# Replacing two triangular inverses through DRAM by products of repeated squares on TensorE, at the start of a recurrent kernel

## Chip, cores, metric

One core of one Trainium2 chip. The metric is the device time of one execution in microseconds (us), median of several runs. Before the prediction the kernel took 842.51 us (three runs, 840.56 to 845.51).

## The reference, cut to what matters

```python
# r, k, v, w, a, b: (4 batches, 8 heads, 768 steps, 40)
for t in range(S):
    y[:, :, t] = np.einsum('bhd,bhde->bhe', rt, state)
    Sa = np.einsum('bhde,bhe->bhd', state, at)
    state_decay = state * wt[:, :, None, :] - np.einsum('bhd,bhe->bhde', Sa, bt)
    state = state_decay + np.einsum('bhd,bhe->bhde', vt, kt)
# y becomes x: (3072 tokens, 320)
h = x @ w_in                                        # 320 x 2048
g = 0.5 * h * (1.0 + erf(h * inv_sqrt2))
out = (g @ w_out).astype(np.float32)                # 2048 x 320
```

The kernel works through the 768 steps in 12 chunks of 64. In each chunk the recurrence becomes products of 64 by 64 matrices and one inverse: with a strictly triangular matrix N of each head and batch (32 of them), it needs T = 1 + N + N² + … + N⁶³. The dense part (x @ w_in, GELU, @ w_out) follows chunk by chunk. The weights arrive in 64 bits and are converted to float32 on the chip, piece by piece.

## The kernel before: the parts concerned

An inverse is made in 32 by 32 blocks. N is stored to DRAM and fetched back with one block a partition, and one engine (VectorE or GpSimd) solves column by column. The result goes through DRAM again, and a *corner* on TensorE joins the blocks.

```python
def start_inverse(c, eng, place=None):
    ...
    for par in range(2):
        nc.sync.dma_start(out=Nb[par * n:(par + 1) * n], in_=blk)
    ...
    def columns():
        for j in range(BL - 1):                      # 31 columns, two instructions each
            ...
            eng.tensor_tensor(t, W[...], Nb[...], ALU.mult)
            eng.tensor_tensor(W[:, :rows, j + 1:], W[:, :rows, j + 1:], t, ALU.add)
            yield
```

Each group of head products is 32 matmuls of 64 by 64 or less, one for each head and batch. They use 64 by 64 corners of the array. On all four corners a group takes 1.1 us at full clock here. So up to four matmuls run side by side. Each float32 matmul leaves two records in the trace, so a group shows as x64:

```python
def mm(o, lhsT, rhs, first=True):
    nc.tensor.matmul(o, lhsT, rhs, start=first, stop=True, skip_group_check=True)
```

The order of each engine is the order of the program. QY is the pair of groups that gives a chunk's outputs and its new state. A *piece* is one of the parts in which the weights are converted: ten of w_in (5 blocks in 2 column halves) and 16 of w_out, the "second weights". The start reads (cut):

```python
make_N(0)
inverse = start_inverse(0, nc.vector)
...
make_N(1)
inverse_1 = start_inverse(1, nc.gpsimd, ...)
...
corner(0); joined(0)
...
first_pieces((2, 3, 4), nc.vector)      # conversion of w_in
...
make_QY(0, 0); make_QY(0, 1); store_inverse(1); outputs(0)
pieces.append(mlp(0))                   # dense part of chunk 0, handed out by fill()
...
corner(1); turn_state(); joined(1)
...
make_N(2); run(start_inverse(2, nc.gpsimd))
```

## Time and profile before

| | before |
|---|---|
| median | 842.51 us |
| span of the profiled execution | 848.1 us |
| first dense product starts | 125.09 us |
| N product of chunk 3 (the *mark*) | 226.37 us |
| from the mark to the end | 621.7 us |

PE is TensorE, DVE VectorE, ACT ScalarE, POOL GpSimd, and SPq the queue that issues the transfers.

Before the first dense product TensorE has a single pause that nothing in the profile ends (start, duration, and in brackets the pause):

```profile
82.90 2.86 PE L96 MATMUL QY<-VR,ks 64*64 64x104 f32 x58 [2.48 <-issue]
```

### The profile page before, as it was taken

Reading aid. Unit: us, or ns where it says so; the run is one execution under the profiler, and the core shown is the slowest. Engines: PE = TensorE matmul, PEld = TensorE weight load, DVE = VectorE, ACT = ScalarE, POOL = GpSimd, SP = SyncE. Lnnn points to the kernel's source line nnn. Section 1 sums busy time; section 2 is a strip of 40 time slices with the busy share of each in tenths; the row PEclk is TensorE's granted clock in tenths of the full one; section 3 lists DMA queues with packets and bytes.
Section 4 is the critical chain, followed back from the end, with each engine's and each line's share of the span. In section 5 each row is a group of like instructions: output and inputs, shape, how many; then the busy total and the mean of one; then the engine's idle time right before and its main releaser. Section 6 shows DMA issues by size and latency. Waiting matters only on the chain.

```text
span 848.1 us, 29196 instructions
## 1 busy us (share of the span) xinstructions
PE 734.3 (87%) x13256; PEld 600.9 (71%) x13256; DVE 295.1 (35%) x459; ACT 222.8 (26%) x257; POOL 311.7 (37%) x778
## 2 busy tenths in 40 slices
PE   4445379685799999999999999998999999989997
PEld 3334368463787887887787877877877877868785
DVE  2765453956223323232232333233233133211100
ACT  2321145222223232223223232331332322202010
POOL 4138000751057075182281281380570750820000
PEclk9975659876899999999899999998999999999999
DMA  7956583382272262532722622722722622020000
GB/s 127 116 104 138 83 125 100 96 143 66 38 121 40 57 100 52 86 65 45 112 38 46 103 55 46 114 39 45 126 46 48 110 52 47 4 53 11 22 12 15
DMA packets 250252, 60.36 MB, mean 71 GB/s; under 512 B 236240, under 2 KB 245968, under 8 KB 250128
## 3 DMA queue, kind: packets, MB, share of 16 engines
q1 hardware_dynamic: 249800, 58.17, 39.5%
q8 instruction: 104, 1.70, 0.9%
q10 hardware_dynamic: 328, 0.33, 0.2%
q14 instruction: 20, 0.16, 0.1%
HBM read 44.30 MB, written 10.22 MB: 64 GB/s over the span
## 4 chain that ended last, share of the span: by engine, by line
PE 65%; DMA 10%; DVE 8%; POOL 6%; SPq 5%; issue 4%; ACT 2%; ACTq 0%; DVEq 0%; POOLq 0%
PE ph L641 22%; PE po L649 17%; PE QY L96 4%; POOL W L461 3%; POOL tmp L459 3%; PE J L96 2%; DMA inv<-W 2%; SPq L608 2%; PE vT_ps L331 2%; PE kT_ps L331 1%; PE saT_ps L96 1%; PE M_ps L96 1%; DMA Nb<-N 1%; PE tn_ps L331 1%; PE RV_ps L96 1%
## 5 line engine op out<-in xcount | busy, mean ns | idle before, releaser
L649 PE MATMUL po<-w_out_sb,gt 128*128 128x320 f32 x768 | 223.8, 445 | 16.3 <-DVE w_out_sb L243 15.2
L641 PE MATMUL ph<-xt,w_in_sb 64*128 64x256 f32 x1920 | 228.4, 390 | 2.0 <-issue 1.8
L459 POOL TENSOR_TENSOR tmp<-W,Nb 128x126 f32<-128x126 f32 (+22 forms) x310 | 114.0, 368 | 281.6 <-DMA Nb<-N 258.1
L641 PEld LDWEIGHTS ph<-xt,w_in_sb 64*128 64x128 f32 x1920 | 188.2, 192 | 27.3 <-issue 4.1
L649 PEld LDWEIGHTS po<-w_out_sb,gt 128*128 128x128 f32 x768 | 144.9, 194 | 80.5 <-DVE w_out_sb L243 21.8
L461 POOL TENSOR_TENSOR W<-W,tmp 128x126 f32<-128x126 f32 (+22 forms) x310 | 123.6, 399 | 24.3
L643 ACT ACTIVATE gt<-ph 128x1024 f32<-128x1024 f32 x48 | 49.1, 1023 | 177.6 <-PE ph L641 177.5
L653 DVE COPY os<-po 128x320 f32<-128x320 f32 x24 | 11.8, 491 | 131.2 <-PE po L649 123.6
L351 POOL TENSOR_TENSOR ks<-k_raw,part 128x640 f32<-128x640 f32 x12 | 22.5, 1875 | 66.0 <-ACT part L323 44.8
L598 DVE TENSOR_TENSOR y<-QY,y 128x512 f32<-128x512 f32 x22 | 15.1, 685 | 74.4 <-PE QY L96 74.4
L96 PE MATMUL J<-L,N 32*32 32x32 f32 x768 | 10.3, 208 | 31.8 <-DVE L L498 31.8
L383 DVE TENSOR_TENSOR VR<-RV_ps,upper 128x1024 f32<-128x1024 f32 x12 | 14.7, 1223 | 58.6 <-PE RV_ps L96 58.6
L96 PEld LDWEIGHTS J<-L,N 32*32 32x32 f32 x768 | 9.1, 120 | 36.5 <-issue 36.4
L383 DVE TENSOR_TENSOR SM<-M_ps,upper 128x1024 f32<-128x1024 f32 x12 | 14.7, 1224 | 56.4 <-PE M_ps L96 56.4
L383 DVE TENSOR_TENSOR A<-A_ps,upper 128x1024 f32<-128x1024 f32 x12 | 14.7, 1223 | 54.9 <-PE A_ps L96 54.9
L96 PE MATMUL cum<-w_raw,cum_m 128*128 128x320 f32 x48 | 19.6, 538 | 15.7 <-ACT w_raw L313 15.7
L236 ACT ACTIVATE power<-power,rebias 128x320 uint32<-128x320 uint32 (+1 forms) x26 | 15.8, 622 | 52.7 <-DVE power L235 42.3
L643 ACT ACT_TABLE_LOAD x11 | 14.1, 1283 | 57.6 <-PE ph L641 57.6
L433 ACT COPY avs<-av 128x640 f32<-128x640 f32 x12 | 8.3, 692 | 73.5 <-PE av L96 73.5
L331 PE MATMUL vT_ps<-ident,v_pad 128*128 128x128 f32 x96 | 16.0, 323 | 12.3 <-DMA v_pad<-in_v_dram 12.3
L362 DVE TENSOR_TENSOR aT<-aT_ps,wpT 128x1024 f32<-128x1024 f32 x12 | 14.7, 1224 | 27.6 <-ACT wpT L360 21.3
L377 DVE COPY vT<-vT_ps 128x1024 f32<-128x1024 f32 x10 | 12.2, 1224 | 34.2 <-PE vT_ps L331 34.2
(123 smaller groups left out, 959.3 us busy)
## 6 DMA issues: line engine op xcount, KB each, us to landing
Nb<-N SPq DMA_DIRECT2D x22, 256.0 KB
w_raw<-in_w_dram SPq DMA_DIRECT2D x24, 160.0 KB
b_raw<-in_b_dram SPq DMA_DIRECT2D x24, 160.0 KB
k_raw<-in_k_dram SPq DMA_DIRECT2D x24, 160.0 KB
a_pad<-in_a_dram SPq DMA_DIRECT2D x24, 160.0 KB
v_pad<-in_v_dram SPq DMA_DIRECT2D x48, 80.0 KB
r_pad<-in_r_dram SPq DMA_DIRECT2D x48, 80.0 KB
out_dram<-os SPq DMA_DIRECT2D x48, 80.0 KB
```

The costliest lines, as they stand in the source:

```text
L96: nc.tensor.matmul(o, lhsT, rhs, start=first, stop=True, skip_group_check=True)
L236: nc.scalar.activation(power, power, ACT.Relu, bias=rebias, scale=8.0)
L331: nc.tensor.transpose(pt[:, g, n], src(g, n), ident)
L351: nc.gpsimd.tensor_tensor(ks[:, :, :, :D], raws.pop((c, "k")), rwv, ALU.mult)
L383: nc.vector.tensor_tensor(to, pt, upper.unsqueeze(1).to_broadcast([P, 2 * G * NP, C]), ALU.mult)
L459: eng.tensor_tensor(t, W[:, :rows, j:j + 1].to_broadcast([P, rows, rest]), Nb[:, j:j + 1, j + 1:].to_broadcast([P, rows, rest]), ALU.mult)
L461: eng.tensor_tensor(W[:, :rows, j + 1:], W[:, :rows, j + 1:], t, ALU.add)
L598: nc.vector.tensor_tensor(y2, Y, y2, ALU.add)
L608: eng.dma_start(out=xt[own + n * i:own + n * (i + 1), NP], in_=xt[other + REST:other + D, i])
L641: nc.tensor.matmul(ph[:, x, s], w_in_sb[half(x), kt, p * P:(p + 1) * P], xt[half(x), kt], start=kt == 0, stop=kt == NK - 1)
L643: nc.scalar.activation(gt[:, 4 * q:4 * q + 4].rearrange("p (s x) t -> p x s t", x=2), ph, ACT.Gelu)
L649: nc.tensor.matmul(po[:, g], gt[:, f, g * P:(g + 1) * P], w_out_sb[:, f], start=f == 0, stop=f == NF - 1)
```

## The change

The intent: the inverses of chunks 0 and 1 stand in front of everything else. Write the same sum as a product, T = (1 + N)(1 + N²)(1 + N⁴)…(1 + N³²), and do it on TensorE, which is half idle there, with no trip through DRAM. The inputs of chunk 1 come at once, and the first weights are loaded and converted by column halves, so that the first dense product needs only the first halves.

```diff
+    def crossed(name, *pairs):
+        o = duo(name).rearrange("p h (n t) -> p h n t", n=NB)
+        for l, r_ in pairs:
+            for n in range(NB):                     # 8
+                for h in range(2):
+                    for s in range(2):
+                        m = s * NB + n
+                        mm(o[half(s), h, n], ident[half(h), half(h)] if l is None else l[half(h), m], r_[half(h), m],
+                           n == 0 and l is pairs[0][0])
+    def straight(name, l, r_, col): ...             # the same on two of the four corners, columns from col on
+    def doubled(c):
+        nc.scalar.copy(UA, crossed("U2", (L1, U1)))
+        nc.vector.tensor_copy(LA, crossed("L2", (U1, L1)))
+        yield
+        nc.vector.tensor_tensor(X, crossed("T1", (None, U1)), every(eye), ALU.add)
+        yield
+        ...                                         # U4 L4, T2, U8 L8, T4, L16, T8
+        nc.vector.tensor_tensor(T[:, :, 16:], straight("T16", LB, T, 16), T[:, :, 16:], ALU.add)
+        nc.scalar.copy(UB[:, :, 32:], straight("Y16", LB, T, 32))
+        nc.vector.tensor_tensor(T[:, :, 32:], straight("T32", LB, UB, 32), T[:, :, 32:], ALU.add)
@@ the program's order, cut
-    make_N(0)
-    inverse = start_inverse(0, nc.vector)
+    make_N(0, False)
+    powers = doubled(0)
+    doubling(1)                                     # steps of it lie between the other groups
...
-    inverse_1 = start_inverse(1, nc.gpsimd, (...))
-    first_pieces((2, 3, 4), nc.vector)
+    first_pieces((0, 1, 2, 3, 4), 0, nc.gpsimd)     # first column halves
...
+    powers = doubled(1)
...
+    first_pieces((4, 0, 1, 2, 3), 1, nc.gpsimd)     # second column halves
...
+    make_saT(1)
     make_N(2)
     run(start_inverse(2, nc.gpsimd))
+    second_pieces(range(NF), nc.vector)
     seconds(1)                                      # the step that finishes the tenth piece of w_in
```

## The prediction

> **What bounds the kernel now.** I read the page's forty slices first, then the busy time in stretches, then each engine's instructions in order of time, with the chain that ended last beside them. A slice is 21.2 us.
>
> ```profile
> PE   4445379685799999999999999998999999989997
> POOL 4138000751057075182281281380570750820000
> ```
>
> From the twelfth slice on TensorE is nine tenths busy or more; before that it is not. The stretches give the size:
>
> ```profile
> 20.00:40.00 20.00, 8.11 (x28) 6.01 (x28) 15.44 (x39) 6.41 (x8) 3.12 (x6) 1.00 1.01 123
> 60.00:80.00 20.00, 9.07 (x322) 8.12 (x325) 10.24 (x15) 4.19 (x7) 17.10 (x38) 0.50 0.65 130
> 80.00:100.00 20.00, 6.09 (x144) 5.46 (x136) 13.22 (x23) 2.95 (x4) 4.31 (x10) 0.67 0.42 74
> 200.00:220.00 20.00, 12.08 (x114) 10.10 (x114) 6.57 (x13) 3.98 (x5) 0.77 (x3) 0.60 0.26 52
> 240.00:260.00 20.00, 20.00 (x485) 17.12 (x482) 5.22 (x7) 7.17 (x8) 16.20 (x42) 1.00 0.59 86
> ```
>
> The second figure is TensorE's busy time. Over the eleven stretches to 220 us it adds up to 132.8, so 87 us are idle; from 226 us on there is nearly nothing to win. I take the start of chunk 3's N product (226.37 us) as the mark: both kernels do the same from there on, some 616 us of the 842.5. So the question is how much earlier the changed kernel reaches this mark.
>
> TensorE's own order shows the waits on the way (start, duration, and in brackets the idle time with what ended it):
>
> ```profile
> 68.64 1.08 PE L96 MATMUL J<-L,N 32*32 32x32 f32 x64 [11.41 <-DVE L L498]
> 100.87 1.94 PE L331 MATMUL vT_ps<-ident,v_pad 128*128 128x128 f32 x8 [12.30 <-DMA v_pad<-in_v_dram]
> 125.09 7.28 PE L641 MATMUL ph<-xt,w_in_sb 64*128 64x256 f32 x40
> 142.75 4.59 PE L641 MATMUL ph<-xt,w_in_sb 64*128 64x256 f32 x40
> 164.84 1.43 PE L649 MATMUL po<-w_out_sb,gt 128*128 128x320 f32 x2 [4.91 <-DVE w_out_sb L243]
> 215.26 1.08 PE L96 MATMUL J<-L,N 32*32 32x32 f32 x64 [5.08 <-DVE L L498]
> 226.37 1.16 PE L96 MATMUL N_ps<-aT,nT 40*64 40x64 f32 x64
> ```
>
> First the inverse of chunk 0 (through DRAM and on VectorE) and chunk 1's late inputs hold it up, then the conversion of the second weights, then chunk 2's inverse coming back from DRAM. The dense block of chunk 0 starts at 125.1. GpSimd's order holds chunk 2's inverse:
>
> ```profile
> 151.38 0.24 POOL L459 TENSOR_TENSOR tmp<-W,Nb 128x31 f32<-128x31 f32 x1 [22.10 <-DMA Nb<-N]
> 181.39 0.36 POOL L461 TENSOR_TENSOR W<-W,tmp 128x16 f32<-128x16 f32 x1
> 299.65 0.24 POOL L459 TENSOR_TENSOR tmp<-W,Nb 128x31 f32<-128x31 f32 x1 [25.82 <-DMA Nb<-N]
> ```
>
> It takes 62 instructions and 30.4 us here, and 28.4 later (299.65 to 328.1). Between the mask of N (done at 143.1) and the first of them lie 8.3 us of store and fetch.
>
> **What the Trainium skill says.** "TensorE: Matmul & The Clock Gate", Part 1, has the array at half clock until about 3.4 us of sustained work, and back there after an idle window of that length. The trace agrees on the fall: after 4.91 us idle a pair of output matmuls takes 1.43 us, after 1.72 us idle 0.81. It agrees less on the rise: at 123 to 129 us some 6 us of unbroken work were needed. The same page, Part 3, says that matmuls on separate strips of the array run at once; 64 records of a 64 by 64 group take 1.1 us warm here and 1.95 cold, thus 17 ns a record. Its table at the top calls GpSimd's queue strictly first in, first out; in the trace nothing overtakes on that engine, and my main argument rests on it. "DMA: Bandwidth & Descriptors", Specifications, wants at least 512 bytes a descriptor for full rate; 236,240 of the 250,252 packets here are smaller, and the first four inputs (1.31 MB) landed by 12.2 us, some 2.3 us each.
>
> **The change, part by part.**
>
> *Removed:* for chunks 0 and 1 the two stores and fetches, 62 VectorE and 62 GpSimd instructions, and the corner products (some 2 us of TensorE each).
>
> *Added:* 18 groups of 32 small matmuls per chunk: 36 x 1.1 = 40 us warm, 70 cold, less 4 for the corners. Each step ends in a copy out of PSUM (1.02 us ScalarE, 1.22 VectorE), and handovers cost under 0.1 us (cum ends 8.82, its copy starts 8.86).
>
> *Chunk 0.* Inputs at 2.3 us each: w of both chunks by 7.8, b, a, k of chunk 0 by 14.7, chunk 1's by 21.6, v and r by 26.2, then 3.1 MB of first weights by about 48. Eight warming matmuls from 3.5 us, then sums and transposes without a gap: the array should be warm by 10. N and L products end near 17.6, their two masks at 19.3. Then the changed order of TensorE, group by group at 1.1 (transposes 0.9): U2, L2, chunk 1's three transposes, T1, U4, L4 end at 28; N, L of chunk 1 at 30; T2 32; k, v, r 35; U8, L8 37; RV, T4, A, L16, T8, av at 45.6. T16, Y16, T32 each wait for a copy, some 2.2 us apiece: sap ends near 54 (before: 74.5). VectorE's conversions between them are the likeliest delay.
>
> *Chunk 1.* From there to the first dense product TensorE has 38 us of groups, with ScalarE 32 us of copies, logs, table loads and conversions in strict order beside it. I allow 5 us for waits: first dense product at **97** (before: 125.1). So 28 us won.
>
> *And lost again.* The ten pieces of first weights now end in two GpSimd instructions each. The order of the changed GpSimd has nine pieces before chunk 2's inverse and the **tenth behind its 62 instructions**. The third dense product needs that piece. So: first dense product 4.5, two groups 2.2, mask 1.4: 105. Plus 8.3 for store and fetch, 28.4 for the inverse, some 2.7 for two instructions on 128 by 512 (from 1.57 for 128 by 640): **144**. Before, the third dense product started at 142.75. The whole lead is gone: TensorE idles some 32 us, from about 112 to 144, and VectorE's second conversion stands behind it too, as it needs the same piece's buffer.
>
> *After it.* Third product 5.5 (half cold) and two QY groups 3.4: chunk 1's QY ends at T = 153 (before 157.0). Then 13.5 of 16 second-weight pieces are still to convert, at 0.32 + 0.32 + 0.48 + 0.48 + 0.49 = 2.1 us: 28.4; state and outputs 5.4, two masks 2.4, a copy 0.8: 37. Their raw data are issued behind the output copies (6.7 us of issue) and chunk 3's loads (7 us), so I add 5: the last piece at T + 42 (before T + 47.5, with 11 pieces left). From there: rest of the third output product, corners, four transposes (3.6), fourth output product (4.5), joining: 11 us, where before it took 22, as three cold transposes (5.5) came after it and the inverse was waited for (5.1). Now the inverse is back long before. Mark at T + 53 = **206**, that is 20 us earlier. 842.5 - 20 = **823 us**.
>
> **The rivals.**
>
> *No stall.* If the tenth piece were done in time, the third product would start near 113, the mark be near 175, and the time near 792. For it: the author meant to hand over a lead of 28 us. Against: program order on GpSimd, which no wait can change. I give it 5%.
>
> *The new matmuls become the bound.* If gaps between dependent steps keep the array cold, chunk 0 ends near 60 and the first dense product near 107; all later marks shift by 10: 833 us. For it: between 100 and 117 us before, cold groups with gaps of 0.7 to 1.4 us stayed cold. Against: the warming matmuls and the interleaved work of the other chunk. 25%.
>
> *Transfers bound the start.* All of chunk 1's inputs go ahead of the weights, and the last weights land near 48, the first of them at 32. Their conversion starts near 45 at the earliest, so this should be hidden; raw data of the second half have 15 us to spare. If not, 5 to 8 us: 830. 10%.
>
> *Faster tail of the prologue.* If the conversions run freely after QY, at VectorE's pace, 5 us less: 818.
>
> **Range and chances.** The limit for 2% is 825.7 us, close to my number. The stall ties the mark to the first dense product: each microsecond by which this comes earlier or later goes through in full. I am unsure of it by some 8 us, of the part after QY by 6. That gives 806 to 838 for 8 in 10. Faster by over 2%: 0.57; within 2%: 0.41; slower: 0.02, as the prologue would have to lose 17 us beyond what it wins.
>
> **What would show it.** The first dense product near 97 us with a gap of about 30 us before the third, ended by a GpSimd instruction that writes the first weights; chunk 2's inverse on GpSimd right before this, unbroken; chunk 0's groups at 1.1 us from 10 us on; sap of chunk 0 near 54; no wait for chunk 2's inverse before its corner; the mark near 206, and the same length after it. I am wrong if the third dense product follows the second by less than 10 us, if the groups of chunk 0 last 1.9 us, or if the conversions after QY take over 48 us, as then they and not the stall set the end of the prologue.

## More of the kernel before

The page's headline, instruction queue and chain of work that ended last.

"Issue" is time in which an engine waited for nothing that the profile shows; q8 is a queue of instructions.

```profile
span 848.1 us, 29196 instructions
...
q8 instruction: 104, 1.70, 0.9%
...
PE 65%; DMA 10%; DVE 8%; POOL 6%; SPq 5%; issue 4%; ACT 2%; ACTq 0%; DVEq 0%; POOLq 0%
```

The page counts 13,256 matmul records and as many weight loads for TensorE. These 26,512 instructions in blocks of 256 are 103.6 blocks, and q8 shows 104 packets of 16 KB (1.70 MB). So q8 carries TensorE's instructions, 256 in a packet, and 128 matmul records with their weight loads use one up.

## The result, and the profile after

| | before | after |
|---|---|---|
| median (same chip) | 843.5 us | 886.58 us |
| span of the profiled execution | 848.1 us | 885.5 us |
| first dense product | 125.09 us | 141.61 us |
| third dense product | 142.75 us | 154.90 us, then again from 188.09 |
| mark | 226.37 us | 268.44 us |
| mark to the end | 621.7 us | 617.1 us |

The ratio after to before is 1.0506, 95% interval 1.0458 to 1.0553: slower by 5%. Every ratio here is the mean time of one kernel's fast runs over that of the kernel before in the same rounds, so it is not quite the ratio of the medians. One of the four runs after was slow (900.84 us) and doesn't count; the profiled one was fast.

From the mark on nothing is lost, so the whole loss lies before it. The page after; the two rows of digits answer to those of the prediction:

```profile
span 885.5 us, 33267 instructions
...
PE   6678769055769999999899999999999998989997
...
POOL 4004213640102714807418247066083480630000
...
q8 instruction: 120, 1.97, 1.0%
...
PE 59%; issue 10%; POOL 9%; SPq 8%; DMA 7%; DVE 5%; ACT 1%; POOLq 0%; DVEq 0%; ACTq 0%
```

TensorE starts busier than before (667876 against 444537), then there is a 0: the eighth slice, where GpSimd shows a 6. And "issue" went from 4% to 10% of the chain. So three questions: what the zero is, what the issue time is, and what happens after the zero. The busy times in stretches (PE, weight loads, DVE, ACT, POOL; then clock, DMA share, GB/s):

```profile
20.00:40.00 20.00, 13.21 (x511) 12.57 (x511) 7.99 (x7) 4.06 (x4) 2.39 (x3) 0.84 0.71 149
60.00:80.00 20.00, 14.69 (x429) 13.87 (x425) 6.34 (x12) 5.66 (x9) 5.08 (x4) 0.67 0.33 60
80.00:100.00 20.00, 14.19 (x593) 13.56 (x590) 8.60 (x11) 7.68 (x12) 8.79 (x8) 0.76 0.46 109
160.00:180.00 20.00, 0.00 (x0) 0.00 (x0) 0.00 (x0) 0.00 (x0) 16.63 (x44) 0.50 0.00 0
```

Between 20 and 100 us TensorE is busy for some 70% of the time. There is work, but no engine in the table is full and neither is the DMA. Some of TensorE's instructions, in order of time, show why (start, duration, and in brackets the idle time and what ended it):

```profile
18.56 0.89 PE L97 MATMUL U<-N,gt 64*64 64x64 f32 x38 [1.55 <-DVE gt L408]
20.93 1.01 PE L97 MATMUL U<-N,gt 64*64 64x64 f32 x26 [1.48 <-issue]
42.07 1.76 PE L97 MATMUL T<-T,ident 64*64 64x64 f32 x51 [5.43 <-issue]
66.50 3.32 PE L97 MATMUL T<-Tt,gt 64*64 64x48 f32 x64 [0.25 <-ACT Tt L519]
79.70 1.95 PE L97 MATMUL sap<-avs,Tt 64*64 64x40 f32 x64 [0.79 <-DVE Tt L525]
116.23 0.85 PE L97 MATMUL A_ps<-aT,kT 40*64 40x64 f32 x42 [1.91 <-issue]
120.66 0.85 PE L97 MATMUL T<-T,LA 64*64 64x64 f32 x41 [2.34 <-issue]
141.61 4.59 PE L731 MATMUL ph<-xt,w_in_sb 64*128 64x256 f32 x40
188.09 5.81 PE L731 MATMUL ph<-xt,w_in_sb 64*128 64x256 f32 x28 [31.62 <-POOL w_in_sb L259]
250.33 1.94 PE L353 MATMUL nT_ps<-ident,nb 128*128 128x128 f32 x8 [7.61 <-DVE nb L372]
```

Three things are to be seen.

First, TensorE pauses *in the middle of a group*: the group U is cut into 38 and 26 records by 1.48 us with nothing to wait for. Before its first dense product it has 16 such pauses, 27.2 us in sum; the kernel before had one of 2.48 us in that part. I counted the records up to each: 220, 475, 603, 731, 985, 1113, 1241, 1368, 1751, 2007, and so on. They lie 128 records apart, or a multiple of it, give or take one that the trace misses: 256 instructions, one packet of q8. (After: 15,326 records with their loads are 119.7 blocks, and q8 has 120.) Where two pauses lie one block apart, the groups behind them start 3.4 to 4.8 us after each other, and once 7.6. The profile has no name for the wait, but its spacing is that of the blocks in which instructions arrive.

Second, the predicted stall: 31.62 us before the third dense product, ended by GpSimd. GpSimd's order at its end:

```profile
158.46 0.24 POOL L550 TENSOR_TENSOR tmp<-W,Nb 128x31 f32<-128x31 f32 x1 [10.50 <-DMA Nb<-N]
...
185.24 0.23 POOL L552 TENSOR_TENSOR W<-W,tmp 128x16 f32<-128x16 f32 x1
185.42 1.27 POOL L258 TENSOR_TENSOR mant<-mant,w_out_sb 128x512 f32<-128x512 f32 x1
186.77 1.26 POOL L259 TENSOR_TENSOR w_in_sb<-mant,power 128x512 f32<-128x512 f32 x1
```

Chunk 2's inverse runs from 158.46 to 185.47, and the tenth piece of w_in stands behind it.

Third, from the end of chunk 1's QY (196.9) to the mark (268.4) pass 71.5 us. The chain of work that ended last shows what holds this stretch (start, duration, what):

```profile
203.57 0.81 SPq L696
...
217.73 0.67 SPq L133
218.45 4.03 DMA spare_raw<-in_moe_w_out_dram
223.97 0.50 DVE w_out_sb L254
```

The issuing queue works from 203.57 to 218.45 on the output copies and chunk 3's inputs. Only then comes the load of the next second weights, and 4.03 us more pass until they land.

### The profile page after: what moved, and what is told of

Its sections match the earlier page's. It is cut to its first block, busy times and chain, and to the rows that moved or that the text cites. A ratio compares the mean times of both kernels' runs of the same rounds, so it can differ in the third digit from the quotient of the medians.

```text
span 885.5 us, 33267 instructions
## 1 busy us (share of the span) xinstructions
PE 768.0 (87%) x15326; PEld 638.4 (72%) x15326; DVE 271.0 (31%) x384; ACT 241.4 (27%) x285; POOL 306.0 (35%) x737
## 4 chain that ended last, share of the span: by engine, by line
PE 59%; issue 10%; POOL 9%; SPq 8%; DMA 7%; DVE 5%; ACT 1%; POOLq 0%; DVEq 0%; ACTq 0%
PE ph L731 20%; PE po L739 16%; POOL W L552 4%; POOL tmp L550 4%; PE QY L97 4%; SPq L133 2%; SPq L699 2%; DMA inv<-W 2%; PE J L97 2%; DMA Nb<-N 2%; PE kT_ps L353 1%; PE T L97 1%; PE tn_ps L353 1%; PE A_ps L97 1%; PE M_ps L97 1%
## 5 line engine op out<-in xcount | busy, mean ns | idle before, releaser
L731 PE MATMUL ph<-xt,w_in_sb 64*128 64x256 f32 x1920 | 225.4, 388 | 32.3 <-POOL w_in_sb L259 31.6
L731 PEld LDWEIGHTS ph<-xt,w_in_sb 64*128 64x128 f32 x1920 | 185.6, 191 | 57.2 <-POOL w_in_sb L259 32.0
L552 POOL TENSOR_TENSOR W<-W,tmp 128x126 f32<-128x126 f32 (+22 forms) x310 | 119.3, 385 | 24.3
L373 POOL TENSOR_TENSOR ks<-k_raw,part 128x640 f32<-128x640 f32 x11 | 19.2, 1744 | 71.0 <-ACT part L345 65.9
L258 POOL TENSOR_TENSOR mant<-mant,w_out_sb 128x512 f32<-128x512 f32 x9 | 11.6, 1284 | 84.1 <-ACT mant L257 84.1
L97 PE MATMUL RV_ps<-rT,vT 40*64 40x64 f32 x768 | 15.0, 229 | 7.6 <-ACT rT L401 5.8
L97 PEld LDWEIGHTS J<-L,N 32*32 32x32 f32 x640 | 6.7, 105 | 20.3 <-issue 20.3
L97 PEld LDWEIGHTS RV_ps<-rT,vT 40*64 40x64 f32 x768 | 13.3, 142 | 11.0 <-ACT rT L401 6.0
L97 PE MATMUL J<-L,N 32*32 32x32 f32 x640 | 7.6, 193 | 15.5 <-DVE L L589 15.5
L97 PEld LDWEIGHTS QY<-VR,ks 64*64 64x64 f32 x768 | 18.3, 137 | 3.6 <-issue 3.6
```

The source lines that it names most:

```text
L373: nc.gpsimd.tensor_tensor(ks[:, :, :, :D], raws.pop((c, "k")), rwv, ALU.mult)
L731: nc.tensor.matmul(ph[:, x, s], w_in_sb[half(x), kt, p * P:(p + 1) * P], xt[half(x), kt], start=kt == 0, stop=kt == NK - 1)
```

## The experiments

Theory A: TensorE's instructions arrive in blocks of 256, one block takes longer than 128 small matmuls take to run, and so the added groups cost their supply time, not their array time. Rival B: the pauses keep the array at half clock, or the added columns are simply too many; this is a cost of the array. Beside both: the stall (C), and the late second weights or the order of copies after QY (D).

All kernels passed the comparison with the reference. The kernel before took 843.07 us (seven runs) beside the first four, 841.86 (eight) beside the next four; its other medians stand with their runs.

### 1. The stall alone

```diff
     make_N(2)
+    convert(0, True)          # finish the tenth piece ahead of the inverse
     run(start_inverse(2, nc.gpsimd))
```

> The changed kernel with one line more: the tenth piece of first weights is finished before chunk 2's inverse is put on GpSimd. Stall theory (the third dense product waits 31.6 us for a GpSimd instruction behind the inverse, 156.5 to 188.1 us): that gap shrinks to under 3 us and the time falls by 25 to 32 us, from 886.6 to 855-862 us, still slower than the 843.5 before. Rival (the stall only takes the place of waits for second weights, which would then appear before the output products): the gap goes, other gaps of 15 us or more come before the output products, and the time falls by under 15 us. Neither touches the first dense product, which stays near 141.6 us.

Measured: 860.61 us, ratio 1.0231 (1.0168 to 1.0294). The 31.6 us are gone, and 26.0 of them show in the median. In this profile the issue pauses came to 35.0 us (one of 7.02), and the first dense product came at 149.6, 8 us later than in the kernel after, though nothing ahead of it was changed; that is where the rest is (more on this spread in experiment 5). The stall was 60% of the loss, and without it the kernel is still 2% slower than before. So C is right, and not enough.

### 2. Fewer instructions for the same columns: the products with the identity

```diff
         for l, r_ in pairs:
+            if l is None:     # one matrix for all: 4 matmuls of 512 columns for 32 of 64
+                for h in range(2):
+                    for s in range(2):
+                        mm(o[half(s), h], ident[half(h), half(h)], r_[half(h), s * NB:(s + 1) * NB], l is pairs[0][0])
+                continue
```

> The changed kernel with the products by the identity (one group in T1, one each in T2, T4, T8) done as 4 matmuls of 512 columns instead of 32 of 64; same result, same columns, 112 matmuls fewer per chunk (448 records in all, 3.5 blocks of 128 records). Instruction supply theory (TensorE pauses with no wait after each 128 records, 16 times before the first dense product, and cannot go faster than about 3.7 us per 128 records in these stretches): the first dense product comes 10 to 14 us earlier than 141.6, and the time falls by as much, to about 874 us. Half clock theory (groups last 1.9 us because the array is throttled, pauses are by-products): the number of instructions does not matter, the first dense product moves by under 4 us.

Measured: 876.40 us, ratio 1.0421 (1.0346 to 1.0497), about 10 us faster than after. The first dense product moved from 141.6 to 131.3. The stall is as long as before (31.9 us), so these 10 us come from the doubling alone: the issue pauses fell from 27.2 to 17.5 us. With the same number of columns, A expects a gain and a cost of the array as such does not.

### 3. Half of the instructions, the same columns, and a wrong result

```diff
-            for n in range(NB):
+            for n in range(0, NB, 2):
-                        mm(o[half(s), h, n], ... l[half(h), m], r_[half(h), m],
+                        mm(o[half(s), h, n:n + 2], ... l[half(h), m], r_[half(h), m:m + 2],
```

> The changed kernel with every crossed product done by 16 matmuls of 128 columns instead of 32 of 64: wrong results on purpose, the same columns through the array, 448 matmuls (896 records, 7 blocks) fewer. Instruction supply theory: first dense product 20 to 28 us earlier than 141.6, pauses labelled issue from 16 to 9 or fewer, time near 862 us. Half clock theory: same columns, same duration per group, first dense product within 4 us of 141.6.

This uses one matrix for two heads and is wrong. (The comparison with the reference passed all the same, so that test says little of the inverse here.) Measured: 864.26 us, ratio 1.0269 (1.0201 to 1.0337), 22 us faster than after with the stall still in it (31.1 us). The first dense product is at 120.3, and the pauses fell from 16 with 27.2 us to 7 with 15.6. This is the largest single effect on the part before the first dense product. A group of 32 records with 128 columns took 1.10 us, as one of 64 with 64 did, so the array had the same to do:

```profile
24.47 1.10 PE L97 MATMUL T<-N,ident 64*64 64x128 f32 x32
```

The pauses make 11.6 of the 21.3 us by which the first dense product moved. The granted clock over 20 to 100 us also rose, from 0.73 to 0.87; how the rest divides, this run doesn't show.

### 4. The supply by itself

The kernel before, with dummy products at its very end: 24 groups of 32 matmuls of 64 columns on four corners, then the same with 128 columns. Nothing else runs, and no data move.

```diff
     fill(1000)
+    bench("bench64", 24, 64)
+    bench("bench128", 24, 128)
```

> The kernel before, with two rows of dummy products after its end, where no transfers run: 24 groups of 32 matmuls of 64 by 64 by 64 on four strips, then 24 groups with 128 columns. They wait for nothing. Instruction supply theory: the first row shows pauses at every 128 records and takes 1.8 us or more per group (43 us or more in all) even at full clock and with idle DMA engines; the second, where the array needs twice as long for as many instructions, shows none and takes about 2.2 us per group. Half clock theory: the first row starts at 1.95 and falls to 1.1 us per group within 10 us, 28 us in all, without pauses.

One look (925.71 us, state unknown, which doesn't matter for durations within it). TensorE in order of time, at its end:

```profile
854.43 2.09 PE L96 MATMUL bench<-w_in_sb 64*64 64x64 f32 x128 [1.65 <-issue]
858.45 2.09 PE L96 MATMUL bench<-w_in_sb 64*64 64x64 f32 x128 [1.93 <-issue]
...
898.31 11.22 PE L96 MATMUL bench<-w_in_sb 64*64 64x128 f32 x384 [0.30 <-issue]
```

and the stretch 850 to 860 us:

```profile
850.00:860.00 10.00, 5.74 (x361) 5.46 (x364) 0.00 (x0) 0.00 (x0) 0.00 (x0) 1.00 0.02 5
```

128 records take 2.09 us at a granted clock of 1.00, then comes a pause, every time. From one start to the next pass 3.47 to 4.02 us. All other engines are idle, and the DMA share of 0.02 is three q8 packets of 16 KB in the 10 us, one for each block. With twice the columns a block has longer to run, and the pauses shrink to 0.30 or vanish (none were expected). This settles what the pauses are: half clock isn't needed for them, dependent copies neither, and the limit is about 256 instructions in 3.5 to 4 us. It doesn't say what the half clock cost in the kernel after. Nor was it tested whether the recording of the profile itself takes part in the pauses.

### 5. Both repairs together

Experiments 1 and 2 in one kernel.

> The changed kernel with both edits: tenth piece ahead of chunk 2's inverse, and the identity products wide. If the stall (886.6 to 860.6) and the supply of instructions (886.6 to 876.4) are independent, their gains add: 850 us (847 to 854), still slower than the 843 before. If the second only shortened the way to the stall, the gain of the pair is less than their sum by some 5 us.

Measured: 842.67 us, ratio 1.0019 (0.9951 to 1.0088), the same as before the change. The wide identity products are worth 18 us here, against 10 with the stall in place. That is more than either forecast allowed (the sum of the two gains, or less). Single sizes are not firmer than this: up to the first dense product, the kernel after and experiments 1 and 6 run the same program, yet their profiles show 27.2, 35.0 and 32.1 us of pauses, and that product starts at 141.6, 149.6 and 142.6. The two kernels with wide products have 17.5 and 13.7 us of pauses and start it at 131.3 and 124.5. The two groups stay apart, but within one the start differs by up to 8 us. So the two repairs together undo the loss, but don't yet give a gain. The part from QY to the mark is as long as ever: 72.3 us in this profile.

### 6. The order after QY

The repaired stall, the fourth dense product ahead of QY, and chunk 2's v and r copies on VectorE as in the kernel before:

```diff
-        copy = nc.scalar.copy if c < 3 else nc.vector.tensor_copy
+        copy = nc.scalar.copy if c < 2 else nc.vector.tensor_copy
     make_M(1)
+    seconds(1)
+    fill()                    # the fourth dense product
     make_y2(1)
-    seconds(2)
+    seconds(1)
     fill()
     second_load(6, 0, spare_raw)
     make_QY(1, 0)
     make_QY(1, 1)
     ...
-    fill()                    # its place before
```

> The kernel with the stall taken out, and the fourth dense product moved ahead of chunk 1's QY as in the kernel before, with chunk 2's v and r copies back on VectorE. Theory: after QY the conversions of the second weights wait behind the state writing, which waits for the fourth dense product (there is one xt buffer), and RV of chunk 2 then waits 7.3 us for a ScalarE copy that stands behind conversions; so the way from the end of QY to the mark (chunk 3's N; 72 us in the stall-free kernel) falls to 60-66 us while the dense product adds 4.5 ahead of QY: 854 to 858 us. Rival (transfers of the second weights set this part): no change beyond 2 us, 859 to 863.

Measured: 858.29 us, ratio 1.0204 (1.0142 to 1.0266): 2 us less than experiment 1, within the intervals of both. From QY to the mark it took 68.5 us instead of 72.2, not the 60 to 66 expected, and these 3.7 us are less than the 4.6 of the dense product that left the stretch. So the order of copies is at most a small part. The chain explains why, here as in the kernel after: the second weights' load stands behind 15 us of issuing (171.16 to 186.41), whichever engine copies.

### 7. When the weights' transfers run

Experiment 1 with the loads of the first weights issued behind chunk 1's v and r.

```diff
-    first_load((0, 1), 0, place(0, 2))      # and three more
     logs(0)
     ...
     load_v(1)
     load_r(1)
+    first_load((0, 1), 0, place(0, 2))      # and three more
```

> The stall-free kernel with the loads of first weights issued behind chunk 1's v and r, so that hardly any transfer runs between 26 and 46 us. If the long pause of TensorE near 36 us (5.4 us in the changed kernel, 7.0 in the stall-free one, 7.5 in the half-count one; others 0.7 to 2.7) comes from the weights' transfers delaying the fetch of instructions, it shrinks to under 2.7 us. If it belongs to the place in the program, it stays at 5 us or more. The time itself may rise by a few us, as the conversions start later.

One look gave 845.87 us (state unknown, clock 0.961), 15 us better than experiment 1. The stretch 20 to 46 us of experiment 1:

```profile
20.00:46.00 26.00, 14.21 (x562) 13.34 (x557) 7.99 (x7) 4.06 (x4) 2.39 (x3) 0.78 0.65 134
```

and with the late loads:

```profile
20.00:46.00 26.00, 19.85 (x893) 18.54 (x892) 10.43 (x9) 8.93 (x9) 2.39 (x3) 1.00 0.34 55
```

The long pause near 36 us fell from 7.02 to 1.59 us, and 893 records were done in place of 562. It looked like a second cause, transfers that slow the supply. The same kernel again, in rounds:

> The same kernel as in the single look before, now timed in rounds, as that one time (845.9 us) has no interval. Theory that the weights' transfers slow the supply of instructions at 26 to 46 us: 843 to 849 us again, against 860.6 us with the loads early. Rival (the single run was a lucky one, the pauses only move): 855 us or more.

Measured: 858.84 us (four fast runs, 852.35 to 863.92), ratio 1.0210 (1.0147 to 1.0272), beside 841.3 of the kernel before. So the single time didn't come again, and the rival stands: in total nothing is won. (The rounds ran on another chip than the single look, so luck isn't told apart from the chip; the kernel before took about the same on both.) The local effect came again, though, and so did its price. The pause near 36 us is 1.59 again, but there are now such pauses where the weights are moving:

```profile
58.00 0.59 PE L97 MATMUL L<-LA,gt 64*64 64x64 f32 x11 [5.97 <-issue]
65.39 0.59 PE L97 MATMUL T<-T,ident 64*64 64x64 f32 x12 [3.70 <-issue]
...
102.41 0.97 PE L97 MATMUL QY<-SM,nb 64*64 64x104 f32 x15 [4.59 <-issue]
```

The longest pause went where the large transfers went: over 52 to 58 us the DMA share is 0.75 here. Over 61.7 to 65.4 it is 0.41, and over the 4.59 us before 102.4 only 0.28, so not every long pause fits. That transfers lengthen the wait for a block is thus likely but not shown, and moving them doesn't save the time. I have no run in which the data transfers alone are taken away.

### 8. A version that spends fewer instructions

Doubling for chunk 0 only, with wide identity products. Chunk 1's inverse goes back to GpSimd, which is idle there, and the first weights' pieces to VectorE. The order after QY is close to that of the kernel before, and three loads of second weights are issued earlier.

```diff
-    make_N(1, False)
+    make_N(1)
+    inverse_1 = start_inverse(1, nc.gpsimd, ...)     # its N in a free block of gt
     ...
     load_v(1); load_r(1)                             # run(inverse_1) ahead of these
-    first_pieces((0, 1, 2, 3, 4), 0, nc.gpsimd)
+    first_pieces((0, 1, 2, 3, 4), 0, nc.vector)
-    powers = doubled(1)                              # and its steps
+    corner(1); turn_state(); convert(1); joined(1)
+    second_load(3, 12); second_load(4, 10); second_load(5, 8)   # earlier
```

> Repeated squares only for chunk 0 (identity products wide), chunk 1's inverse on GpSimd through DRAM as in the kernel before, all first-weight pieces on VectorE, dense products ahead of QY. Supply theory: about 1150 records fewer than the wide kernel before the first dense product, 9 blocks of 3.7 us: first dense product at 95 to 110 us (125.1 before), no stall of the third, time 815 to 832 us, faster than before by 1.5 to 3%. Rival (chunk 1's inverse or its way through DRAM then sets the start of the first dense product, as the inverse of chunk 0 did before): first dense product at 115 us or later, time 838 or more.

Measured: 825.86 us, ratio 0.9806 (0.9735 to 0.9877): faster than both kernels, though by 2% or not stays unclear. There are 7 issue pauses with 12.9 us before the first dense product, which comes at 113.9: beyond the 95 to 110 of the supply theory and just short of the rival's 115, though the time is as forecast. From QY to the mark it takes 61.9 us, instead of 68.5 in experiment 6, where the fourth dense product is also ahead of QY (71.5 in the kernel after, where it isn't). Second weights and the issuing queue are no longer among the large items of the chain in that stretch. As several things differ, this points to the late loads as the cause there, but doesn't isolate it.

### 9. The same, with late loads of the first weights

```diff
-    first_load((0, 1), 0, place(0, 2))      # and three more
     ...
     inverse_1 = start_inverse(1, nc.gpsimd, ...)
+    first_load((0, 1), 0, place(0, 2))      # and three more
```

> The mixed kernel with the loads of the first weights issued behind the store and fetch of chunk 1's N instead of ahead of them. Theory (transfers of the weights slow the supply of instructions, and they hold back chunk 1's N on the issuing queue): the pause of 6.1 us near 39 us shrinks to below 3, GpSimd's wait for chunk 1's N falls from 31.6 us to below 15, chunk 1's corner product J no longer waits 9 us; first dense product at 100 to 106 us instead of 113.9, the mark about 195 to 200, time 812 to 820 us. Rival (the pauses merely move to where the weights now run, and the conversion of the first weights then starts late): first dense product at 110 to 116, time 823 to 828 us as for the mixed kernel.

Measured: 818.49 us, ratio 0.9716 (0.9655 to 0.9778), beside 841.3 of before. Run again on another chip:

> The mixed kernel with late weights once more, on the same chip as the one with the corner moved, so that the two can be compared directly: ratio to the kernel before 0.966 to 0.978 again.

819.79 us, ratio 0.9761 (0.9690 to 0.9832), beside 842.5. This is the best version here, 2.4 to 2.8% under the kernel before. The time is as forecast, much of its path is not. The first dense product came at 109.3 (100 to 106 expected) and the mark at 203.1 (195 to 200). The pause near 39 us shrank to 2.9 us, but one of 5.1 us came near 49 us, as the rival has it. GpSimd's wait for N fell from 31.6 to 18.0 us, not below 15, and that bought nothing at the corner product J, which waits as long as before (the mixed kernel had 8.96):

```profile
104.15 1.08 PE L97 MATMUL J<-L,N 32*32 32x32 f32 x64 [8.97 <-DVE L L595]
```

So GpSimd's inverse is not what J waits for, though I had read the mixed kernel's trace that way.

### 10. What J waits for

```diff
     make_av(1)
+    corner(1)
     sums(2)
     scale(2)
     convert(1)
-    corner(1)
     turn_state()
```

> The mixed kernel with late weights, and chunk 1's corner products put ahead of chunk 2's sums and of one conversion step in the program. Theory (J waits for VectorE's own order: the transposition L stands behind two conversions and behind copies that wait for ScalarE, not for GpSimd's inverse, which is back 20 us earlier): the wait of 9.0 us before J falls below 2, the first dense product comes at 100 to 105 us instead of 109.3, the time falls by 4 to 8 us against the kernel with late weights on the same chip. Rival (the dense products are set by the conversion of the first weights, so the wait turns up again before the first or third dense product): first dense product or third at the same place as before, time the same within 2 us.

Measured: 828.96 us, ratio 0.9866 (0.9820 to 0.9912), some 9 us *slower* than experiment 9 on the same chip. The theory fell: J came at 103.3, nearly where it was. Its transposition L now names another releaser:

```profile
102.48 0.71 DVE L595 STREAM_TRANSPOSE L<-Tt 128x512 f32<-128x512 f32 x1 [7.26 <-DMA Tt<-inv]
```

GpSimd was done at 69.2 us, but the store of the inverse is issued at 84.45, behind chunk 2's inputs and weight loads, and its fetch at 99.68, behind chunk 0's output copies. In experiment 9 the fetch is issued at 98.58, and L starts at 103.30. With the 2.8 us from issue to L that it took here, that fetch had landed near 101.4 (an estimate), and VectorE's conversions ended at 102.7: about 1 us apart, so removing either alone wins next to nothing. And as the sums of chunk 2 now stood behind J on TensorE, the conversions and a GELU behind them came later too, and a new wait of 7.61 us appeared after the first dense product. I didn't run the repair that this suggests, an earlier store and fetch.

## Why the prediction was wrong

I take its own sum, the mark, from the profiled execution after.

| step | predicted, us | measured, us | difference |
|---|---|---|---|
| first dense product | 97 | 141.6 | +44.6 |
| from there to the third, or its continuation | 47 | 46.5 | -0.5 |
| from there to the end of chunk 1's QY | 9 | 8.8 | -0.2 |
| from there to the mark | 53 | 71.5 | +18.5 |
| mark | 206 | 268.4 | +62.4 |

The mark came 42 us later than before, instead of 20 earlier, and 842.5 + 42 is within 3 us of the measured median.

**Right: the stall.** Named with its cause, 32 us from about 112 to 144; measured 31.62 us, 44 us later. Its terms hold one by one: from the first dense product to the mask of N 8.0 us (8.1 predicted), store and fetch 8.9 (8.3), the inverse 27.0 (28.4), the two instructions behind it 2.6 (2.7). Taking it away moved the time by 26 us (experiment 1). Nearly right too: the length from the mark on, the same but for 4.6 us; the "616" takes the mark of one execution from the median of others, and the profile itself has 621.7.

**Wrong: the step to the first dense product.** The step that failed reads "From there to the first dense product TensorE has 38 us of groups … I allow 5 us for waits: first dense product at **97**", and the term behind it "36 x 1.1 = 40 us warm". The 1.1 us came from groups that ran one at a time in the kernel before, between other work. One such group is 128 instructions, half a block; thirty in a row outrun the supply. The sum had no term for instructions at all. Measured in its place: 16 issue pauses, 27.2 us. A block of 256 instructions needs 3.5 to 4.0 us alone on the chip (experiment 4), two groups of the prediction were to take 2.2. An estimate from this: the 36 added groups are 18 blocks, 62 to 72 us in place of 40, thus 22 to 32 us more.

The Trainium skill has the block: "Runtime: NRT & Kernel Launch", section "Instruction fetch mechanics", gives refills of 16 KiB blocks of 256 instructions, and calls the cost of a boundary mostly hidden. The trace agrees on the block (119.7 blocks, 120 packets), but not that it is hidden here (27.2 us). A warning was in the trace of before as well, the one pause of 2.48 us at QY, which I took for a detail.

A second mis-sized term is in the same sum: T16, Y16 and T32 use two of the four corners of the array. I gave them 1.1 us each like the others. They took 3.3 to 3.6 for chunk 0 and 2.0 to 2.1 for chunk 1, together 16.7 for six instead of 6.6: 10 us more. Some 4.5 of these are the half clock at which chunk 0's three ran (10.6 us, chunk 1's 6.1), the rest the two corners. The remaining 7 us of the 44.6 are found by subtraction; cold groups and small waits would be in them. The clock of 0.67 between 60 and 80 us is the rival "new matmuls become the bound", which I gave 25% and 10 us. That rival had the right place but not the main reason: the half clock is there, but experiment 4 pauses at full clock, and halving the instructions with the same columns brought 21 us at the first dense product. What the half clock cost apart from the supply, no run isolates. One reading behind it was wrong: where the prediction says "some 6 us of unbroken work were needed", the trace of before has TensorE busy without a break from 120.8 us and the clock at 0.50 until about 130.5, some 10 us.

**Wrong: "Mark at T + 53".** The last piece of second weights was done at T + 52.5 instead of T + 42. That is beyond the 48 us which the prediction named as a sign of being wrong. One term was cut short: I counted 6.7 us of issue for the output copies and 7 for chunk 3's loads, and then added only 5, as I took the data to be ready in part. The issue took 14.9 us and the landing 4.0, and the chain runs through all of it. From that piece to the mark it took 19.0 us instead of 11: TensorE stood 7.61 us before chunk 3's last transposes, for a copy that VectorE made only behind the last piece, so the third output product came after them whole (16 records, 5.8 us), where the prediction had only a rest of it. The kernel before has the same issuing (14.2 us) and needed 69.4 us for this stretch, the kernel after 71.5, so nothing was won where I had 16 us. What I first blamed, the order of ScalarE's copies, is refuted as the main cause by experiment 6. The chain and the shorter stretch of experiment 8 point to the late loads, but no run changes them alone, so this cause stays open.

**The rivals.** "Transfers bound the start" was off the point in the form I gave it. Moving the weights' transfers moves the pauses, not the time (experiment 7); in the mixed kernel, where it also brings chunk 1's N forward, it is perhaps worth some 6 us (0.9806 to 0.9716 and 0.9761, on three chips and with intervals that overlap). "No stall" and "faster tail of the prologue" did not come true.

## What to carry to other kernels

Count instructions beside busy time: a stretch of small matmuls, 128 records with their weight loads in less than about 3.5 us, was bound by the supply of instructions here, so fewer and wider matmuls beat more of them even with the same columns. Pauses at constant counts of instructions with no releaser are its sign, and a single one in the trace of before is a warning. And a wait whose releaser is removed shows the next one: before moving work ahead of a wait, find everything that ends there, down to the order of the queue that issues the transfers.

## What the Trainium skill lacked or had wrong

- "Runtime: NRT & Kernel Launch", section "Instruction fetch mechanics": a boundary of 256 instructions is called mostly hidden, and fetching faster than issuing. Here 128 records of 64 columns (64 float32 matmuls) with their weight loads ran in 2.09 us and were followed by 1.38 to 1.93 us of pause, at full clock with idle data queues; a block costs 3.47 to 4.02 us.
- The same section gives TensorE room for 2048 instructions, and elsewhere only two lines of 16 KiB. No trace here shows a long reserve: the kernel after pauses for the first time after 220 records of matmuls, or some 440 instructions, and then every 128 or a multiple.
- "TensorE: Matmul & The Clock Gate", Part 3, promises concurrency from packing on separate corners of the array, and has nothing on supply. Packed fourfold, 64 by 64 products of 64 columns run at 16 ns a record (2.09 us for 128) but are supplied at 27 to 31 ns (3.47 to 4.02 us for 128); with 128 columns pauses shrink to 0.30 us or vanish.
- No page speaks of data transfers that lengthen the fetch of instructions. Here the longest pause moved with the transfers: 7.02 us near 36 us at a DMA share of 0.65 over 20 to 46 us, 1.59 us at 0.34 with the loads elsewhere, and 5.97 us where they then ran. As one of 4.59 us came at a share of only 0.28, this is likely, not shown.
